# The first slot of the experts: its first weights loaded and halved during attention

## Chip, cores and metric

One NeuronCore of a Trainium2 chip runs the program. The metric is the device time in microseconds, the median of several runs.

## The reference

Attention with a memory (B = 4, H = 8, S = 576, D = 64), an expert layer that gives each of 2304 tokens to one of 8 experts (512 to 1024 to 512), and a dense layer (512 to 2048 to 512), all fp32:

```python
local = softmax(causal(q @ k.T / 8)) @ v
mem_out = (phi(q) @ M_prev) / (phi(q) @ z_prev + 1e-6)
x = sigmoid(beta) * mem_out + (1 - sigmoid(beta)) * local   # -> (2304, 512)
e_idx = argmax(x @ w_gate)                                  # one expert a token
y = gate_w * sigmoid(x @ w_output_gate)[e] * (relu(x @ w1[e]) @ w2[e])
h = y @ w_in
out = (h - tanh(h)) @ w_out
```

## The kernel before

Each fp32 product is made of three matmuls: both factors are halved into a high and a low part (`split`, L48: ScalarE casts the high part, L50, and VectorE subtracts it, L51), and high by high, high by low and low by high are added up in PSUM.

*Attention.* 16 pairs: four batches of four pairs of heads. In a pair PE (TensorE) transposes q and k (`tq`, `tk`, `tt`), makes scores (`sc`, and `sct` for the last query block, L448), and later the transposes of the weights (`g`, `ta`, `tb`), the products with v (`l`) and the projection to the tile `xb` that is stored to the table `xd`; VectorE masks the scores and takes their row maxima (`a`, `nm`, L455), ScalarE takes the exponentials (L476, L487). The order on each engine is not that of the code. Every operation is put into a `Plan` with a due time, its cost on each engine that can do it, and what it reads and writes; a list scheduler walks through them by due time and writes out one fixed order for each engine. The due times come from tables: `DUE` by kind of operation, shifted by `PERIOD` a pair, `ROUTE` for the steps of the router, `DUE0` for what is done once: the gates (VectorE, L110 to L124), the 0/1 patterns and number rows of the router (`laterrt`, VectorE and GpSimd, L727 to L773), the gate weights `w160`.

*Router.* After each batch, `Router.batch` picks an expert for each token from the logits in `acc` (`mx` to `os`, L833 to L848), and counts them (`cb`, `cs`; the matmuls `rp`, L887 to L891). After the third batch, `Router.first_slot` (names `e_...`) takes the fullest expert so far, its number `e_e` (L973), gathers 256 of its tokens and halves them into `xh_first`, `xl_first`. The rest, with the last batch, is done in `Router.slots` (L1019), a generator of some ten short chunks that make the tables of all slots: the first (up to `nF`, L1060) counts the slots of each expert, the next ones write the token list of slot 0 and its expert number `ei` (L1103), the last write other tables.

*Experts.* Slot e (256 tokens, list made in attention), then twelve more slots. A slot has eight steps of 128 inner features. Step f: 12 matmuls into `ph`, Relu on ScalarE (`hh`), its remainder on VectorE (`hl`, L1301), 12 matmuls into `y`. `run_slots` (L1189) drives it: `first` and `parts2` halve a step's pieces of w1 (`ah`, `al`) and w2 (`bh`, `bl`), `load` issues two DMAs of 512 KB each for every two steps on SyncE, `ahead` keeps `first` two steps ahead. `between`, a function of the main program, runs after each step: it takes the next chunk of `Router.slots` and, later, a piece of the dense layer's conversions. In slot e, step 0:

```python
            if s.first and f == 0:
                nc.scalar.copy(s.wh, r)
                nc.gpsimd.tensor_tensor(out=s.wl, in0=r, in1=s.wh.bitcast(F32), op=ALU.subtract)
```

The number of its expert is read into SyncE by a register load that stands ahead of the last stores of `xb`; the loads of its weights stand behind those stores.

Of the kernel before, what the change touches and what calls it, by code (L numbers as in the profile page):

```python
# [276 lines left out]
DUE = {
    "mx": (-371.1, -38.4, -63.2, -4.7, -23.8, -10.4, -17.1, -329.2), "kt": (-356.8,), "nrm": (-319.8,),
    "phi": (-319.7,), "qtt": (-218.6,), "pt": (-193.0,), "ptt": (-174.7,),
    "ex": (-97.7, -29.7, -360.9, -178.0, 9.4, 9.1, -54.4, -78.3), "lt": (-66.1, -9.5), "mxt": (-65.1,),  # L280
    "cp": (-60.8, -194.3, -30.0, -48.9, -29.0), "tpt": (-49.1,), "sdt": (-48.6,), "qt": (-47.4,),
    "new": (-45.7,), "sm": (-45.7,), "loadq": (-36.0,), "consts": (-30.0,), "qexp": (-29.5,), "loadk": (-20.7,),
# [6 lines left out]
}  # L289

DUE0 = {"constsM": 33.9, "constsz": 16.3, "laterM": -165.5, "latergates": 6.8, "laterrt": 17.1, "laterw160": -25.5, "laterzeros": 23.6}

# [895 lines left out]

def run_slots(tc, c, pm, ps, rt, slots, w1, w2, x2, between):  # L1189

# [54 lines left out]
    def first(s, f):  # L1245

        nm = f"{s.n}_{f}"
        load()
        r1 = raw[s.n, f - f % 2][0]
        if s.nl == 2:  # L1250
            s.wh, s.wl = wtile(f"ah_{nm}", "wh", [P, 4, P]), wtile(f"al_{nm}", "wl", [P, 4, P])
            r = r1[:, :, (f % 2) * P:(f % 2 + 1) * P]
# [12 lines left out]

    def parts2(s, f, j):
        nonlocal used
        nm = f"{s.n}_{f}"
# [433 lines left out]
```

## Time and profile before

| what | us |
|---|---|
| median of 3 runs | 983.3 (982.25 to 983.88) |
| profiled execution | 983.37 |
| its span | 981.5 |
| attention, to the last write of `xb` | 0 to 263.38 |
| slot e, to the end of `xl` of slot 0 | 263.38 to 299.64 |
| other slots and dense layer | 299.64 to 981.5 |
| busy: PE, DVE, ACT, POOL | 924.2, 807.3, 655.7, 128.3 |

PE is TensorE's matmuls, PEld its weight loads, DVE VectorE, ACT ScalarE, POOL GpSimd, SP SyncE, SPq its DMA issues. In a timeline a row gives the start in the span, the duration, the engine, the line, the operation, output <- input, the shape, the number of equal operations, and in brackets how long the engine was idle before it and what it waited for. In a table of stretches each engine has its busy time and its instructions; the clock is the share of full speed (2.4 GHz) that TensorE was granted.

### The profile page before, as it was taken

The numbers are of one execution on the slowest core, as the hardware profiler recorded it, in microseconds if no ns is written. First come the engines' busy times: TensorE is split into PE (matmuls) and PEld (weight loads), VectorE is DVE, ScalarE is ACT, GpSimd is POOL, SyncE is SP. The second block draws the span as 40 slices with busy tenths as digits, with TensorE's granted clock in tenths as the row PEclk, the third lists the DMA queues.
The fourth block names the chain that finished last, engine by engine and source line by source line (L and its number), as shares of the span: only waits on it lengthen the run. The fifth ranks groups of instructions, "written<-read, shape, count | busy, mean of one in ns | idle before, by whom it ended". The sixth has DMA issues, their size and how long they took to land. (4 is left out here: it accounts for less than half of the span.)

```text
span 981.5 us, 16678 instructions
## 1 busy us (share of the span) xinstructions
PE 924.2 (94%) x5661; PEld 759.2 (77%) x5661; DVE 807.3 (82%) x1908; ACT 655.7 (67%) x1441; POOL 128.3 (13%) x145
## 2 busy tenths in 40 slices
PE   5899999999599999999999899999999999999996
PEld 3567666666489989989998777777887888788895
DVE  4566777868589989988888789999889888988896
ACT  4577777776346676676768467776667666665784
POOL 2433233322230001000000000001001000100000
PEclk9799999999889999999999899999999999999999
DMA  5133433431378987888988201001000000100000
GB/s 126 26 81 83 100 88 83 104 84 36 102 223 253 291 299 229 266 284 265 307 263 268 89 2 43 22 1 44 1 1 33 11 1 1 44 1 1 12 33 22
DMA packets 139117, 103.60 MB, mean 106 GB/s; under 512 B 85776, under 2 KB 120592, under 8 KB 139024
## 3 DMA queue, kind: packets, MB, share of 16 engines
q1 hardware_dynamic: 135680, 91.88, 32.0%
q0 software_dynamic: 3200, 10.58, 3.3%
q8 instruction: 46, 0.75, 0.3%
q14 instruction: 47, 0.39, 0.1%
q10 hardware_dynamic: 144, 0.00, 0.0%
HBM read 92.93 MB, written 9.51 MB: 104 GB/s over the span
## 5 line engine op out<-in xcount | busy, mean ns | idle before, releaser
L1469 PE MATMUL og<-wouth,fgl 128*128 128x512 f32 x288 | 115.4, 401 | 8.0 <-DVE fgl L1480 7.9
L1469 PE MATMUL og<-woutl,fgh 128*128 128x512 f32 x288 | 114.8, 399 | 0.0
L1553 ACT ACTIVATE fu<-fph 128x512 f32<-128x512 f32 (+1 forms) x80 | 44.4, 555 | 104.9 <-PE fph L1520 81.2
L1469 PE MATMUL og<-wouth,fgh 128*128 128x512 f32 x288 | 113.5, 394 | 0.2
L1520 PE MATMUL fph<-fxh,fwh 128*128 128x512 f32 (+1 forms) x256 | 93.8, 369 | 4.8 <-ACT fxh L50 4.8
L1520 PE MATMUL fph<-fxh,fwl 128*128 128x512 f32 (+1 forms) x256 | 93.2, 367 | 0.0
L1520 PE MATMUL fph<-fxl,fwh 128*128 128x512 f32 (+1 forms) x256 | 92.9, 365 | 0.0
L476 ACT ACTIVATE a<-a,nm 128x128 f32<-128x128 f32 (+3 forms) x128 | 71.6, 567 | 21.4 <-DVE nm L455 21.4
L1487 POOL DMA_INDIRECT out_dram<-ob,olist x18 | 18.9, 1049 | 458.8 <-ACT ob L1485 246.9
L1555 DVE SCALAR_TENSOR_TENSOR fs<-fs,fu 128x512 f32<-128x512 f32 (+1 forms) x80 | 50.9, 637 | 29.7 <-ACT fs L1554 29.3
L1469 PEld LDWEIGHTS og<-wouth,fgl 128*128 128x128 f32 x288 | 54.3, 189 | 25.0 <-DVE fgl L1480 13.3
L51 DVE TENSOR_TENSOR bl<-r,bh 128x512 fp32r<-128x512 f32 x96 | 64.5, 686 | 11.1 <-ACT bh L50 10.7
L1308 PE MATMUL y<-hh,bh 128*128 128x256 f32 x256 | 71.8, 280 | 0.0
L1308 PE MATMUL y<-hh,bl 128*128 128x256 f32 x256 | 71.4, 279 | 0.0
L1308 PE MATMUL y<-hl,bh 128*128 128x256 f32 x256 | 71.4, 279 | 0.0
L455 DVE CUSTOM_DVE_ANT_0 a<-sc,cm 128x128 f32<-128x128 f32 (+3 forms) x128 | 57.5, 487 | 8.9 <-PE sc L435 8.6
L51 DVE TENSOR_TENSOR al<-r,ah 128x512 fp32r<-128x512 f32 x96 | 64.4, 685 | 0.1
L1469 PEld LDWEIGHTS og<-wouth,fgh 128*128 128x128 f32 x288 | 54.3, 189 | 12.7 <-ACT fgh L1475 1.4
L1469 PEld LDWEIGHTS og<-woutl,fgh 128*128 128x128 f32 x288 | 54.3, 189 | 12.1 <-DVE woutl L51 0.5
L1566 DVE TENSOR_TENSOR ft<-fph,ft 128x512 f32<-128x512 f32 (+1 forms) x80 | 50.9, 636 | 11.6 <-ACT ft L1564 11.2
L1300 ACT ACTIVATE hh<-ph 128x256 fp32r<-128x256 f32 x64 | 24.7, 385 | 52.6 <-PE ph L1295 52.6
L1520 PEld LDWEIGHTS fph<-fxh,fwh 128*128 128x128 f32 x256 | 48.9, 191 | 13.9 <-ACT fxh L50 5.7
(372 smaller groups left out, 2797.8 us busy)
## 6 DMA issues: line engine op xcount, KB each, us to landing
r<-in_moe_w_dram SPq DMA_DIRECT2D x96, 512.0 KB
d<-in_moe_w_in_dram SPq DMA_DIRECT2D x16, 512.0 KB
d<-in_moe_w_out_dram SPq DMA_DIRECT2D x16, 512.0 KB
qr<-in_q_dram SPq DMA_DIRECT2D x32, 128.0 KB
kr<-in_k_dram SPq DMA_DIRECT2D x32, 128.0 KB
vr<-in_v_dram SPq DMA_DIRECT2D x32, 128.0 KB
xd<-xb SPq DMA_DIRECT2D x32, 128.0 KB
r_e<-in_moe_w_dram SPq DMA_DIRECT2D x8, 512.0 KB
```

What stands on the lines that cost most here:

```text
L51: nc.vector.tensor_tensor(out=lo, in0=src, in1=hi.bitcast(F32), op=ALU.subtract)
L455: nc.vector.tensor_tensor_reduce(out=y, in0=x, in1=mask, scale=-0.125, scalar=init, op0=ALU.add, op1=ALU.min, accum_out=out)
L476: nc.scalar.activation(a, a, AF.Exp, bias=s.nm[:, o:o + 1], scale=-1.0, accum_out=s.sum[:, i, j:j + 1])
L1300: nc.scalar.activation(hh, hv, AF.Relu)
L1308: nc.tensor.matmul(s.y[d // 2][:, d % 2, :], st[:, d * P:(d + 1) * P], mv, start=f == 0 and m == 0 and d % 2 == 0, stop=f == 7 and m == 2, ...
L1469: nc.tensor.matmul(og[ci][t], st[:, ts], mv, start=f == 0 and m == 0, stop=f == 15 and m == 2)
L1487: sc = nc.gpsimd.indirect_dma_start(out=out, out_offset=bass.IndirectOffsetOnAxis(ap=perm[:, i:i + 1], axis=0), in_=ob, in_offset=None).ins
L1520: nc.tensor.matmul(h, st[:, k, :], xp[ci, k][o], start=m == 0, stop=m == 11)
L1553: nc.scalar.activation(u, h, AF.Square)
L1555: nc.vector.scalar_tensor_tensor(out=s, in0=s, scalar=KA, in1=u, op0=ALU.add, op1=ALU.mult)
L1566: nc.vector.tensor_tensor(out=th, in0=h, in1=th, op=ALU.subtract)
```

## The change

A new class `Early` makes 12 tiles in a pool `wide` that lies in the memory of the later tiles `wout` of the dense layer: w1 and w2 of inner features 0 to 255 of slot e's expert, and their high and low parts. As soon as the expert number is known, SyncE loads them (four DMAs of 256 KB), and four casts and four subtracts halve them before attention ends. `run_slots` makes no pieces for steps 0 and 1 of slot e and takes `pre.a`, `pre.b`; the halving on GpSimd is gone. `between` is not called ahead of slot e and does nothing after its step 0, so that the chunks of the router start after step 1 and end two steps later, the last two in slot 0. All due times are new.

```diff
-PERIOD = 19.44
-ROUTE = 1.48
+PERIOD = 20.2
+ROUTE = 1.35
 DUE = {
...
-DUE0 = {"constsM": 33.9, "constsz": 16.3, "laterM": -165.5, "latergates": 6.8, "laterrt": 17.1, "laterw160": -25.5, "laterzeros": 23.6}
+DUE0 = {"constsM": 28.5, "constsz": 3.9, "laterM": -151.2, "latergates": -23.5, "laterrt": -12.9, "laterw160": -28.9, "laterzeros": 27.7}
...
+            if nm == "e_f6":
+                plan.add(at, f"e_load_{b}", (("SP", 2.0),), lambda e: pre.load(rt.v["e"]), r=w, w=["ew"], lat=6.0)
+                for i, (e_, d_, f_) in enumerate(pre.steps):
+                    plan.add(NPAIR * B * PERIOD + 7.0 + 0.5 * i, f"e_w{i}_{b}", ((e_, d_),), lambda e, f=f_: f(), r=["ew"] + ([f"ew{i - 1}"] if i % 2 else []), w=[f"ew{i}"])
...
+class Early:
+    def __init__(self, tc, pool, w1, w2):
...
+        self.r = [[t(f"er{n}_{f}", F32, (P, 4, P) if n == 1 else (P, DM)) for f in range(2)] for n in (1, 2)]
+        self.a = [[t(f"ea{a}_{f}", F32R, (P, 4, P)) for a in "hl"] for f in range(2)]
+        self.b = [[t(f"eb{a}_{f}", F32R) for a in "hl"] for f in range(2)]
+        self.steps = []
+        for f in range(2):
+            for x, (h, l) in ((self.r[0][f], self.a[f]), (self.r[1][f], self.b[f])):
+                self.steps.append(("ACT", 0.6, lambda x=x, h=h: nc.scalar.copy(h, x)))
+                self.steps.append(("DVE", 0.7, lambda x=x, h=h, l=l: nc.vector.tensor_tensor(
+                    out=l, in0=x, in1=h.bitcast(F32), op=ALU.subtract)))
+    def load(self, t):
+        e = nc.sync.value_load(t[0:1, :], min_val=0, max_val=E - 1)
+        for f in range(2):
+            nc.sync.dma_start(self.r[0][f], self.w1[bass.ds(e, 1), :, f * P:f * P + P].rearrange("a (k p) f -> p (a k) f", p=P))
+            nc.sync.dma_start(self.r[1][f], self.w2[bass.ds(e, 1), f * P:f * P + P, :].rearrange("a p f -> p (a f)"))
...
-    pieces = [(s, f) for s in slots for f in range(0, 8, 2)]
+    pieces = [(s, f) for s in slots for f in range(0, 8, 2) if f or not s.first]
...
+        if s.first and f < 2:
+            s.w1[f] = pre.a[f]
+            return
...
-            if s.first and f == 0:
-                nc.scalar.copy(s.wh, r)
-                nc.gpsimd.tensor_tensor(out=s.wl, in0=r, in1=s.wh.bitcast(F32), op=ALU.subtract)
-            else:
-                split(nc, s.wh, s.wl, r)
+            split(nc, s.wh, s.wl, r)
...
+        if s.first and f < 2:
+            return pre.b[f]
...
-    between(slots[0], 0, -1, None, None)
...
-            if i == 0 or i == 1 and f % 2:
+            if i == 0 and f or i == 1 and f % 2:
```

How this moves instructions, at three places. First VectorE around the first masks of attention (`a`, `nm`; `ptc` and `ir` are the last constants of the router). Before, in front of pair 1's first mask:

```order
L751 CAST thr<-thr_i 128x18
L766 CAST ptc<-io_t 128x40
L767 MEMSET ptc 64x4x2
L771 CAST ir<-io_r 128x128
L370 SCALAR_TENSOR_TENSOR ph_181<-qr_165,ph_181 128x640
L455 ISA a_0_140,nm_137<-sc_1_357,cm 128x128
L455 ISA nm_137 128x1
```

With the change, in front of pair 0's first mask (the gates `sel` to `ft` and the other constants stand directly ahead of these rows, and nothing but the setting up of masks and gate weights ahead of those):

```order
L754 CAST thr<-thr_i 128x18
L769 CAST ptc<-io_t 128x40
L770 MEMSET ptc 64x4x2
L774 CAST ir<-io_r 128x128
L416 TENSOR_TENSOR qtt_264<-tt_262,bm 128x128
L454 ISA a_1_144,nm_140<-sc_0_280,cm 128x256
L454 ISA nm_140 128x1
```

Gates and router constants have moved from between pair 0 and pair 1 to ahead of pair 0. Second, SyncE's queue at the end of attention (`xd<-xb` are the stores of the last batch, `r_e` slot e's weights as they are loaded). Before:

```order
L1196 TENSOR_LOAD e_e
L1196 ISA x2
L643 DMA xd<-xb_118 128x4x64 x2
L643 DMA xd<-xb_118 64x64 x2
L643 DMA xd<-xb_118 128x4x64 x2
L643 DMA xd<-xb_118 64x64 x2
L1240 ISA
L1240 DMA r_e_3334<-in_moe_w_dram 128x4x256
L1242 ISA
```

With the change (`er_0`, `er_1` are the raw pieces of steps 0 and 1):

```order
L1201 ISA
L1201 DMA er_0_87<-in_moe_w_dram 128x4x128
L1202 ISA
L1202 DMA er_0_89<-in_moe_w_dram 128x512
L1201 ISA
L1201 DMA er_1_88<-in_moe_w_dram 128x4x128
L1202 ISA
L1202 DMA er_1_90<-in_moe_w_dram 128x512
L1227 TENSOR_LOAD e_e
L1227 ISA x2
L642 DMA xd<-xb_133 128x4x64 x2
L642 DMA xd<-xb_133 64x64 x2
```

The four early loads stand ahead of the last stores; behind those the first `r_e` load is now that of step 2. Third, VectorE around the count `cb` and the running count `cs` of the last batch, which the list-making chain starts from (`os` is the chosen output gate logit, `rank` and `rlo` belong to the chain). Before:

```order
L853 TENSOR_REDUCE cb_3350<-oh 128x8
L848 TENSOR_REDUCE os_3272<-oe_3268 128x5
L854 TENSOR_TENSOR cs<-cs,cb_3350 128x8
L897 TENSOR_TENSOR rs_3364<-rp_3355,oh 128x40
L898 TENSOR_REDUCE rank<-rs_3364 128x5
L899 CAST ri_3367<-rank 128x5
L900 TENSOR_SCALAR rj_3369<-ri_3367 128x5
L901 TENSOR_SCALAR ri_3367<-ri_3367 128x5
L902 CAST rhi<-rj_3369 128x5
L903 CAST rlo<-ri_3367 128x5
```

With the change:

```order
L851 TENSOR_REDUCE os_3308<-oe_3304 128x5
L1333 SCALAR_TENSOR_TENSOR hl_e_3396<-ph_e_3382,hh_e_3395 128x256
L51 TENSOR_TENSOR al_e_3413<-r_e_3370,ah_e_3412 128x512
L1333 SCALAR_TENSOR_TENSOR hl_e_3417<-ph_e_3399,hh_e_3416 128x256
L856 TENSOR_REDUCE cb_3434<-oh 128x8
L857 TENSOR_TENSOR cs<-cs,cb_3434 128x8
```

The subtract `al_e` (step 2's weights) and two remainders `hl_e` (steps 0 and 1) now stand ahead of the count `cb`, and so of all chunks of the router.

## Rows read from the trace of the kernel before

**Rows 1.** Stretches: us, busy PE, PEld, DVE, ACT, POOL, clock, DMA share, GB/s.

```profile
16.81:34.88 18.07, 12.22 (x45) 6.46 (x46) 11.28 (x61) 8.25 (x25) 8.86 (x34) 0.76 0.37 83
34.88:50.60 15.72, 15.72 (x95) 10.74 (x95) 9.37 (x37) 10.79 (x31) 5.14 (x4) 0.84 0.11 24
50.60:236.61 186.01, 184.20 (x1303) 125.71 (x1303) 138.41 (x547) 140.77 (x409) 59.01 (x42) 1.00 0.38 84
263.38:299.64 36.26, 28.44 (x230) 27.02 (x231) 31.63 (x103) 15.31 (x33) 9.13 (x10) 0.86 0.77 241
299.64:322.80 23.16, 22.84 (x208) 22.59 (x207) 20.35 (x40) 15.70 (x33) 2.75 (x4) 1.00 0.77 237
```

**Rows 2.** Timeline of PE, first pairs: start, duration, operation, [idle before it <- releaser].

```profile
16.81 2.02 PE L448 MATMUL sct<-kt,qtt 128*128 128x512 f32 x2
...
32.83 1.64 PE L435 MATMUL sc<-kt,qt 64*128 64x384 f32 x2 [3.91 <-DVE nm L455]
...
50.60 1.08 PE L448 MATMUL sct<-kt,qtt 128*128 128x512 f32 x2
```

**Rows 3.** Stretches around the fall of the clock, columns as in rows 1.

```profile
19.40:26.26 6.86, 4.93 (x31) 2.86 (x29) 6.26 (x39) 5.92 (x16) 0.83 (x8) 1.00 0.45 101
26.26:34.88 8.62, 4.71 (x11) 2.15 (x11) 4.49 (x22) 2.33 (x9) 6.15 (x24) 0.50 0.14 31
```

**Rows 4.** Timelines of ACT, SP's queue and DVE at the start.

```profile
6.20 0.74 ACT L367 ACTIVATE ph<-qr 128x640 f32<-128x640 f32 x1
...
4.02 0.59 SPq L135 DMA_DIRECT2D w<-in_moe_w_gate_dram  x1
...
6.64 1.15 SPq L352 DMA_DIRECT2D kr<-in_k_dram  x2
...
20.57 0.16 DVE L114 TENSOR_SCALAR g<-g 128x8 f32<-128x8 f32 x1
...
22.09 0.46 DVE L124 COPY ft<-g 128x8 f32<-128x8 f32 x5
...
25.32 0.11 DVE L735 CAST ie<-io_e 128x8 f32<-128x8 int32 x1
...
29.16 0.23 DVE L771 CAST ir<-io_r 128x128 f32<-128x128 int32 x1 [0.21 <-POOL io_r L769]
```

**Rows 5.** Timeline of PE, rank matmul of batch 0.

```profile
117.13 0.19 PE L887 MATMUL rp<-ohb,tri 128*128 128x40 bf16 x1 [0.61 <-DVE ohb L847]
```

**Rows 6.** Stretch before the last write of `xb`, and timeline of DVE there.

```profile
244.00:263.38 19.38, 15.33 (x113) 11.94 (x109) 8.72 (x31) 7.46 (x18) 5.55 (x7) 0.91 0.32 74
...
245.57 0.14 DVE L973 TENSOR_SCALAR e_e<-e_fm 128x1 int32<-128x1 f32 x1
```

**Rows 7.** Timelines of SP's queue and ACT, first weights of slot e.

```profile
265.79 0.40 SPq L1240 DMA_DIRECT2D r_e<-in_moe_w_dram  x1
...
269.24 0.62 ACT L1254 CAST ah_e<-r_e 128x512 fp32r<-128x512 f32 x1 [5.89 <-DMA r_e<-in_moe_w_dram]
```

**Rows 8.** Timeline of DVE in slot e.

```profile
266.78 0.22 DVE L853 TENSOR_REDUCE cb<-oh 128x8 f32<-128x40 f32 x1
...
270.21 0.15 DVE L1060 COPY nF<-end 128x1 f32<-128x1 f32 x1
271.52 0.69 DVE L51 TENSOR_TENSOR bl_e<-r_e,bh_e 128x512 fp32r<-128x512 f32 x1 [1.15 <-ACT bh_e L50]
...
274.21 0.43 DVE L1301 SCALAR_TENSOR_TENSOR hl_e<-ph_e,hh_e 128x256 fp32r<-128x256 f32 x1 [1.40 <-DMA r_e<-in_moe_w_dram]
...
294.21 0.57 DVE L1125 TENSOR_TENSOR rn<-rn,va 128x400 f32<-128x400 f32 x1
...
295.71 0.68 DVE L51 TENSOR_TENSOR bl_e<-r_e,bh_e 128x512 fp32r<-128x512 f32 x1
...
297.25 0.82 DVE L794 TENSOR_TENSOR list_eq<-tk,ir 128x640 bf16<-128x640 f32 x1
298.35 1.29 DVE L51 TENSOR_TENSOR xl<-xt,xh 128x512 fp32r<-128x512 f32 x2 [0.28 <-ACT xh L50]
```

More of the change, by code (lines that the diff above doesn't have):

```diff
@@ L273, with attention @@
 QORDER = (1, 3, 2, 0)
-PERIOD = 19.44
-ROUTE = 1.48
+PERIOD = 20.2
+ROUTE = 1.35
 DUE = {
[L278 to L282, printed above, removed]
[6 rows of a table removed]
-}
-DUE0 = {"constsM": 33.9, "constsz": 16.3, "laterM": -165.5, "latergates": 6.8, "laterrt": 17.1, "laterw160": -25.5, "laterzeros": 23.6}
-def attention(tc, c, pl, ps, src, M_prev, z_prev, rt):
+    "phi": (-111.9,), "ex": (-102.0, -50.1, -50.1, -62.7, 9.7, 9.5, -102.1, -14.1), "xw": (-90.6, 26.0),
+    "cp": (-88.9, 7.5, -12.7, -45.5, -46.0), "ptt": (-87.6,), "qt": (-82.1,), "pt": (-68.5,), "new": (-67.4,),
+    "mxt": (-66.6,), "sct": (-61.0,), "loadq": (-49.3,), "qtt": (-46.7,),
+    "mx": (-44.9, -43.4, -32.7, -70.7, -89.3, -15.8, -25.6, 13.8), "lt": (-42.3, -44.3), "sdt": (-39.6,),
+    "ktt": (-34.9,), "tpt": (-31.9,), "loadk": (-31.1,), "consts": (-30.0,), "qexp": (-29.8,), "mv": (-15.0,),
+    "tq": (-14.8,), "tp": (-13.3,), "pz": (-12.1,), "tk": (-12.1,), "tt": (-11.7,), "kt": (-11.1,),
+    "cb": (-9.0,), "avM": (0.4,), "sc0": (0.4,), "qmin": (0.5,), "nrm": (5.0,), "sc2": (5.1,), "loadv": (5.2,),
[3 rows of a table added]
+}
+DUE0 = {"constsM": 28.5, "constsz": 3.9, "laterM": -151.2, "latergates": -23.5, "laterrt": -12.9, "laterw160": -28.9, "laterzeros": 27.7}
+def attention(tc, c, pl, ps, src, M_prev, z_prev, rt, pre):
     nc = tc.nc
@@ L1171, with t @@
 AH2 = 0
+class Early:
+    def __init__(self, tc, pool, w1, w2):
+        nc = self.nc = tc.nc
+        def t(name, dt, shape=(P, DM)):
+            return pool.tile(list(shape), dt, tag="wout", bufs=17, name=name)
+        self.w1, self.w2 = w1, w2
+        self.r = [[t(f"er{n}_{f}", F32, (P, 4, P) if n == 1 else (P, DM)) for f in range(2)] for n in (1, 2)]
[8 more added lines that the diff above has]
+    def load(self, t):
+        nc = self.nc
+        e = nc.sync.value_load(t[0:1, :], min_val=0, max_val=E - 1)
+        for f in range(2):
+            nc.sync.dma_start(self.r[0][f], self.w1[bass.ds(e, 1), :, f * P:f * P + P].rearrange("a (k p) f -> p (a k) f", p=P))
+            nc.sync.dma_start(self.r[1][f], self.w2[bass.ds(e, 1), f * P:f * P + P, :].rearrange("a p f -> p (a f)"))
 class Slot:
@@ L1186, in __init__, with run_slots @@
         self.w = self.nl * P
-def run_slots(tc, c, pm, ps, rt, slots, w1, w2, x2, between):
+def run_slots(tc, c, pm, ps, rt, slots, w1, w2, x2, between, pre=None):
     nc = tc.nc
@@ L1430, with ffn @@
 C3, GA, AL, KA = -0.018684760036080127, -2.6849726608097573, -0.09139710496091785, 6.635977108247196
-def ffn(tc, c, bp, pf, ps, x2, win, wout, perm, out, cst, rest):
+def ffn(tc, c, wp, pf, ps, x2, win, wout, perm, out, cst, rest):
     nc = tc.nc
@@ L1533, in ffn @@
         if 0 < i < 17:
-            vl = bp.tile([P, DM], F32R, tag="wout", bufs=17, name=f"woutl_{i - 1}")
+            vl = wp.tile([P, DM], F32R, tag="wout", bufs=17, name=f"woutl_{i - 1}")
             split(nc, wouth[:, i - 1, :], vl, wout[i - 1])
@@ L1608 @@
     rt = Router(tc, c, rp, xd)
+    wp = ctx.enter_context(tc.tile_pool(name="wide", bufs=1, side="right", reuse_waits="tile"))
+    pre = Early(tc, wp, w1, w2)
     with ExitStack() as st:
@@ L1612 @@
         make_consts(tc, c, pl, beta, w_gate, w_ogate)
-        late = attention(tc, c, pl, ps, (q, k, v), M_prev, z_prev, rt)
+        late = attention(tc, c, pl, ps, (q, k, v), M_prev, z_prev, rt, pre)
     ps = early.enter_context(tc.tile_pool(name="mps", bufs=4, space=PSUM, reuse_waits="tile"))
@@ L1617 @@
     win = [bp.tile([P, 4, P], F32, name=f"win_{f}") for f in range(16)]
-    wout = [bp.tile([P, DM], F32, tag="wout", bufs=17, name=f"wout_{f}") for f in range(16)]
+    wout = [wp.tile([P, DM], F32, tag="wout", bufs=17, name=f"wout_{f}") for f in range(16)]
     cst = bp.tile([P, 2], F32, name="cst")
@@ L1657 @@
         with tc.manual_schedule():
-            run_slots(tc, c, pm, ps, rt, stat, w1, w2, x2, between)
+            run_slots(tc, c, pm, ps, rt, stat, w1, w2, x2, between, pre)
             for _ in order:
@@ L1669 @@
         with tc.manual_schedule(engines={nc.tensor.engine, nc.vector.engine, nc.scalar.engine}):
-            ffn(tc, c, bp, pf, ps, x2, win, wout, rt.perm, out, cst, [units[j] for j in (28, 30, 27, 29, 31)])
+            ffn(tc, c, wp, pf, ps, x2, win, wout, rt.perm, out, cst, [units[j] for j in (28, 30, 27, 29, 31)])
 _INS = ["q", "k", "v", "M_prev", "z_prev", "beta", "moe_w_gate", "moe_w_output_gate",
```

9 rows, old and new, of the table DUE are left out of this document.

## Prediction

> **What bounds the kernel now.** I read the stretches first (busy time of each engine between two marks of the program), then TensorE's timeline, then VectorE's, and the queue of SyncE where a load is late. All times are of one profiled execution: 983.37 us, of which 981.5 are the span and 1.87 lie around it; the median of the three runs is 983.3, so the sum needs no correction. A difference of 0.2% (2 us) is about what a measurement of this kernel can tell from none.
>
> Attention is a loop of 16 head pairs. The 128x512 matmuls `sct`, two in each pair, mark its beat. From the third `sct` (50.60) to the sixteenth (236.61) PE is busy 184.20 of 186.01 us: PE is the bound, and only 1.81 us could be won by waiting less [rows 1]. The two pairs before it are different. From the first `sct` (16.81) to the second (34.88) PE works 12.22 of 18.07 us at a mean clock of 0.76, and the next pair takes 15.72 without a gap at 0.84 [rows 1]. So the start holds 5.85 us of waiting, of which 3.91 is one wait for VectorE's row maxima `nm` [rows 2], and PE runs at half clock (1.2 of 2.4 GHz) in part of it: 0.50 from 26.26 on [rows 3]. Matmuls before 19.4 are also slow: the first `sct` took 2.02 us, the later one 1.08 [rows 2].
>
> The other loose place is slot e, the first 256 tokens of the experts. From the last write of `xb` (263.38) to the end of slot 0's first halving (299.64) VectorE works 31.63 of 36.26 us and PE 28.44 at a clock of 0.86 [rows 1]: VectorE is the bound there. After that, in slot 0, PE is busy 22.84 of 23.16 and VectorE 20.35 [rows 1].
>
> **The change part by part.** *The order of the start.* The 3.91 us wait comes from what VectorE does before pair 1's first mask: the gates (20.57 to 22.55, 2.0 us), then the router's constants, which go back and forth with GpSimd from 25.32 to 29.39 (4.07 us) [rows 4]. The new order puts both ahead of pair 0's first mask. There VectorE has nothing else: the gate's exponential can follow ScalarE's first `ph`, which ends at 6.94 [rows 4], so gates and constants run from about 7.1 to 7.1 + 2.0 + 4.07 = 13.2. At that time PE still waits for its own input: the first k was issued at 6.64, behind four loads of gate weights that begin at 4.02 [rows 4]; now it goes ahead of them, 2.6 us earlier. PE's chain from k to the first `sct` could end 2.6 us sooner, VectorE's 13.2 plus its copy `qtt` allows about 14.8: I take 14.8, that is 2.0 sooner.
>
> From the first to the second `sct`: of 12.22 us busy, 18.07 x 0.24 x 2 = 8.7 us of the stretch ran at half clock. Less the wait of 3.91, 4.8 us of matmuls were slow; at full clock they take 2.4. The 2.0 us by which the pair starts earlier now lie before 19.4, where matmuls are slow, and cost 1.0. Of the three small waits (1.94 together) I keep one, 0.7. So 12.22 - 2.4 + 1.0 + 0.7 = 11.5, and the second `sct` comes at 26.3. The next pair had 15.72 x 0.16 x 2 = 5.0 us at half clock; without that 15.72 - 2.5 = 13.2, third `sct` at 39.5 in place of 50.60: **-11.1**. Bounds: if PE runs at half clock as long as before, 13.6 us more, 6.8 of it are given back (-4.3); if no wait stays, -12.
>
> What keeps the clock up? The rows show only that it fell to 0.50 at 26.26, after 6.86 us in which PE was busy 4.93 with three short waits, and ahead of the long one [rows 3]. The Trainium skill, "TensorE: Matmul & The Clock Gate", "HAM oscillation — how this bites in real kernels", blames waits between groups of matmuls for the fall. By it the denser start holds the clock and -11.1 stands; by the row alone the clock may fall again without a long wait, and -4.3 is the sum's term. I take -11.1, since the new stretch lacks the waits, and keep the other as a rival.
>
> *Router operations of batches 0 to 2.* They cost PE a wait for `ohb` of about 0.6 us each [rows 5]. The new due times spread them otherwise. At most the whole idle 1.81 us goes [rows 1], at least nothing: **-1.0**.
>
> *Early weights.* Four loads of 256 KB go out on SyncE as soon as the expert is known, 245.57 [rows 6], behind the value register and ahead of the last `xb` stores, which wait for VectorE anyway. Four casts of 0.62 us on ScalarE and four subtracts of 0.69 on VectorE follow. From 244 to 263.38 VectorE works 8.72 of 19.38 us and ScalarE 7.46 [rows 6]: 2.8 and 2.5 us more fit. I cost them at **0**; without that cover they would cost up to 2.8.
>
> *Slot e.* Count from the last `xb` write. Before, the first load of weights went out at +2.4 behind the `xb` stores, and ScalarE's cast began at +5.86 [rows 7]; everything of slot e began there. Now steps 0 and 1 need no load, so PE may begin at about 0. But step 2's weights still stand behind the same stores and arrive at +5.9: cast +6.5, subtract `al` +7.2. VectorE's queue holds this `al` between `hl` of step 0 and `hl` of step 1, ahead of the count `cb`. So the list-making chain, which ran from 266.78 to 270.36 (3.58 us) beside the wait, now follows it: +7.2 + 0.3 + 3.6 = +11.1 for `nF`, where it was +7.0 [rows 8]. From `nF` to `xl` it took 298.35 - 270.36 = 27.99. Out of this go two waits for weights, 1.15 and 1.40; two steps' `bl`, `al`, `hl` at 1.54 a step (295.71 to 297.25); and two chunks of list-making that now lie in slot 0, 1.50 (294.21 to 295.71) and 0.82 [rows 8]. 27.99 - 2.55 - 3.08 - 2.32 = 20.0, so `xl` ends at 11.1 + 20.0 + 1.29 = +32.4. The number of slot 0's expert is now made two steps later, and a load takes 3.45 us from issue to cast [rows 7]; I add 1.4 for waiting on it: +33.8 against +36.26 before: **-2.4**. So most of PE's head start of six us is lost to VectorE. Bounds: -6.5 if only PE's start counts, +4 if the list chain (3.6) finds no cover and the load wait is double.
>
> *Slot 0.* Two chunks, 2.32 us of VectorE, join 20.35 busy of 23.16 [rows 1]: between 0 and +2.3, value **+1.2**.
>
> *Clock in slot e.* PE waits between steps 1 and 2 for about as long as it did before step 0, and 36.26 x 0.14 x 2 = 10.2 us of this stretch were at half clock already [rows 1]. A slower stretch may show behind VectorE: **+1.0**, from 0 to +6.
>
> The sum is -11.1 - 1.0 - 2.4 + 1.2 + 1.0 = -12.3, so 983.37 - 12.3 = **971.1 us**. With its terms' nearer bounds this case reaches from 966 to 976.
>
> **The rivals.** *B, the clock falls all the same at the start.* For it: the fall at 26.26 came without a long wait [rows 3]. Against: PE has fewer gaps. The start's term is then -4.3 and the time 977.9; in the worst case, half clock from the first `sct` to 40, it is -1.5 and 980.7. *C, slot e runs on a half clock.* Its PE work, 28.44 less half of 10.2, is 23.3 us at full and 47 at half clock; steps 2 to 7 at half need 35 us after +7.2, against the 26.6 that VectorE takes. Most of that excess, +6, gives 977. For it: the long PE wait now cuts slot e in two. Against: VectorE leaves PE the slack. *D, slower: the new order makes PE wait in every pair.* The period in the planner was raised from 19.44 to 20.2 and all due times differ; a cast or mask that comes late in one pair is late in 13. It decides from 12.3 / 13 = 0.95 us a pair; today the wait is 1.81 / 13 = 0.14 [rows 1]. At 1.25 a pair the time is 971.1 + 16.3 = 987.4. Against: the mix of copies on ScalarE and VectorE stays nearly the same, and VectorE's busy share in this stretch is only 138.41 of 186.01 [rows 1]. *E, it does not do what it says.* The early weights help nothing, since VectorE bounds slot e, and the constants wait for something else at the start: 983.
>
> **How the numbers follow.** Forecast 0.58, B 0.20, C 0.09, D 0.08, E 0.05. The range takes in the forecast and B and C but for their far ends: 966 to 980.5. Faster by over 0.2%: forecast, B, C, 0.87; within 0.2%: E, 0.05; slower: D, 0.08.
>
> **What the profile after would show.** The third `sct` near 39.5, no wait of 3.91 for `nm`, and a granted clock near 1.00 between 26 and 40 (B: 0.50). About 14.2 us from `sct` to `sct` later (D: over 15). The four early casts and subtracts in the gap before the last `xb`. In slot e PE's first `ph_e` about at the last `xb` write, a wait for `hl` or `al` of some 3 us near +4 to +7, and `xl` ending near +34 (C: PE clock 0.5 until +20). The prediction is wrong if the third `sct` comes after 46, or if slot 0 begins later than +36 after the last `xb`.

## The result, and the profile after

The changed kernel takes 973.75 us (median of 4 runs, 971.69 to 974.65) where the kernel before takes 983.39 (982.25 to 983.88): a ratio of 0.9908, 95% interval 0.9894 to 0.9922, or some 9 us less. The profiled execution took 971.69 us, its span 969.8. That is 2 us below the median, at a mean clock of 0.990 where the three other runs have 0.982 to 0.988; the readings below go by marks inside the profiles.

First the start. TensorE's timeline with the change, to be read against [rows 2]:

```profile
14.19 1.65 PE L434 MATMUL sc<-kt,qt 64*128 64x384 f32 x2 [2.73 <-DVE nm L454]
15.77 2.07 PE L447 MATMUL sct<-kt,qtt 128*128 128x512 f32 x2
...
24.17 0.98 PE L498 MATMUL g<-idf,a 128*128 128x128 f32 x7 [0.95 <-ACT a L475]
...
25.93 1.13 PE L447 MATMUL sct<-kt,qtt 128*128 128x512 f32 x2
...
39.14 1.12 PE L447 MATMUL sct<-kt,qtt 128*128 128x512 f32 x2
```

and the stretches between the first, second and third `sct`, up to the sixteenth, and slot e (columns as in [rows 1]):

```profile
15.77:25.93 10.16, 9.21 (x46) 5.77 (x45) 8.14 (x32) 7.15 (x24) 4.47 (x4) 1.00 0.69 157
25.93:39.14 13.21, 13.21 (x95) 8.81 (x93) 9.35 (x36) 10.27 (x30) 4.80 (x9) 1.00 0.22 49
39.14:223.69 184.55, 183.84 (x1307) 125.81 (x1305) 146.04 (x544) 143.28 (x414) 59.65 (x43) 1.00 0.38 85
252.61:288.37 35.76, 27.93 (x221) 26.69 (x221) 27.37 (x92) 12.47 (x27) 7.83 (x9) 0.91 0.61 194
```

The third `sct` begins at 39.14 (before 50.60). The 3.91 us wait for `nm` of pair 1 is gone; what is left is 2.73 us ahead of the first `sct`, where VectorE now makes the router's constants, and 0.95 behind it. The granted clock is 1.00 from 15.77 to 39.14, where it was 0.76 and 0.84 [rows 1]. Up to about 19 us this record says too much, before as after: the first `sct` took 2.07 us, as long as one at 0.50 in e3 below (2.08), the third 1.12. The loop after it is 1.46 us shorter (184.55 against 186.01), and the wait for the rank matmul fell from 0.61 [rows 5] to 0.21; it comes three times in the loop, once a batch:

```profile
105.55 0.19 PE L890 MATMUL rp<-ohb,tri 128*128 128x40 bf16 x1 [0.21 <-DVE ohb L850]
```

Then the end of attention, first PE, then GpSimd:

```profile
241.82 0.47 PE L568 MATMUL l<-idf,p 128*128 128x128 f32 x1 [2.75 <-POOL p L555]
...
238.04 1.18 POOL L961 DMA_INDIRECT e_xg<-xd,e_li  x1 [11.47 <-DMA er<-in_moe_w_dram]
239.53 0.95 POOL L961 DMA_INDIRECT e_xg<-xd,e_li  x1 [0.30 <-issue]
240.50 1.26 POOL L555 TENSOR_TENSOR p<-ph,gn 128x640 f32<-128x640 f32 x1
```

PE waits 2.75 us for GpSimd's last `p`, which stands behind both gathers of slot e's tokens. From the sixteenth `sct` to the last `xb` write it takes 28.92 us, where it took 26.77 (236.61 to 263.38).

Slot e, VectorE's timeline, then the load and the cast that it waits for, to be read against [rows 7, 8], and PE's first matmul:

```profile
255.66 0.41 DVE L1333 SCALAR_TENSOR_TENSOR hl_e<-ph_e,hh_e 128x256 fp32r<-128x256 f32 x1
259.31 0.69 DVE L51 TENSOR_TENSOR al_e<-r_e,ah_e 128x512 fp32r<-128x512 f32 x1 [3.24 <-ACT ah_e L50]
259.92 0.42 DVE L1333 SCALAR_TENSOR_TENSOR hl_e<-ph_e,hh_e 128x256 fp32r<-128x256 f32 x1
260.25 0.21 DVE L856 TENSOR_REDUCE cb<-oh 128x8 f32<-128x40 f32 x1
...
264.01 0.15 DVE L1063 COPY nF<-end 128x1 f32<-128x1 f32 x1
...
283.89 0.69 DVE L51 TENSOR_TENSOR al<-r,ah 128x512 fp32r<-128x512 f32 x1 [2.29 <-ACT ah L50]
...
287.68 0.69 DVE L51 TENSOR_TENSOR xl<-xt,xh 128x512 fp32r<-128x512 f32 x1 [0.16 <-ACT xh L50]
...
255.02 0.39 SPq L1271 DMA_DIRECT2D r_e<-in_moe_w_dram  x1
...
258.66 0.62 ACT L50 CAST ah_e<-r_e 128x512 fp32r<-128x512 f32 x1 [4.40 <-DMA r_e<-in_moe_w_dram]
...
252.10 0.38 PE L1327 MATMUL ph_e<-xh_first,eah 128*128 128x256 f32 x1 [0.58 <-DVE xl_first L1019]
```

PE's first matmul of slot e in the kernel before:

```profile
269.91 0.58 PE L1295 MATMUL ph_e<-xh_first,ah_e 128*128 128x256 f32 x1 [2.49 <-ACT ah_e L1254]
```

PE's first `ph_e` begins at 252.10, 0.5 us before the last `xb` write (252.61); before, it came 6.5 us after it. But VectorE waits 3.24 us for step 2's cast, whose load went out at +2.4 as before, and only then comes the count `cb` and the list chain: `nF` ends at +11.6. At the end of slot e it waits 2.29 us for the first weights of slot 0. `xl` ends at +35.8, 0.5 us earlier than before (+36.26).

The marks of both traces together (us; `x<-y_e` is the copy that ends slot e, the dense layer begins with its first `fph`):

| mark | before | after | shift |
|---|---|---|---|
| first, second `sct` | 16.81, 34.88 | 15.77, 25.93 | -1.0, -9.0 |
| third `sct` | 50.60 | 39.14 | -11.5 |
| sixteenth `sct` | 236.61 | 223.69 | -12.9 |
| last `xb` write ends | 263.38 | 252.61 | -10.8 |
| `x<-y_e` | 299.59 | 289.50 | -10.1 |
| copy that ends slot 0 | 327.20 | 318.49 | -8.7 |
| dense layer begins | 560.9 | 553.1 | -7.8 |
| end of the span | 981.5 | 969.8 | -11.7 |

So attention's order gained 12.9 us, 5.1 of them were given back between the sixteenth `sct` and the dense layer, and the dense layer, whose code is the same, became 3.9 us shorter. Of these 3.9, 2.4 lie in its steady stretch (258.6 and 256.1 us, see e8) and 1.3 in the stretch ahead of that (97.3 and 96.0 us at a mean clock of 0.96 and 0.97). The latter takes 96.0 to 97.7 us in the fourteen profiles here, in no order that follows the edits, so this part counts as scatter.

### The profile page after: what moved, and what is told of

The parts are those of the page before. It is cut to its first block, busy times and chain, and to the rows that moved or that the text cites. A ratio compares the mean times of both kernels' runs of the same rounds, so it can differ in the third digit from the quotient of the medians.

```text
span 969.8 us, 16684 instructions
## 1 busy us (share of the span) xinstructions
PE 916.9 (95%) x5661; PEld 757.7 (78%) x5661; DVE 814.7 (84%) x1905; ACT 657.3 (68%) x1445; POOL 127.5 (13%) x144
## 5 line engine op out<-in xcount | busy, mean ns | idle before, releaser
L1500 PE MATMUL og<-woutl,fgh 128*128 128x512 f32 x288 | 112.4, 390 | 0.0
L475 ACT ACTIVATE a<-a,nm 128x256 f32<-128x256 f32 (+3 forms) x128 | 70.4, 552 | 18.4 <-DVE nm L454 18.3
L1500 PEld LDWEIGHTS og<-wouth,fgh 128*128 128x128 f32 x288 | 54.1, 188 | 11.5 <-ACT fgh L1506 1.5
L1500 PEld LDWEIGHTS og<-woutl,fgh 128*128 128x128 f32 x288 | 54.1, 188 | 11.1 <-DVE woutl L51 0.5
L454 DVE CUSTOM_DVE_ANT_0 a<-sc,cm 128x256 f32<-128x256 f32 (+3 forms) x128 | 57.4, 485 | 5.6 <-PE sc L434 4.6
L50 ACT CAST ah<-r 128x512 fp32r<-128x512 f32 x96 | 58.2, 624 | 4.9 <-DMA r<-in_moe_w_dram 4.9
```

The costliest lines, as they stand in the source:

```text
L50: nc.scalar.copy(hi, src)
L454: nc.vector.tensor_tensor_reduce(out=y, in0=x, in1=mask, scale=-0.125, scalar=init, op0=ALU.add, op1=ALU.min, accum_out=out)
L475: nc.scalar.activation(a, a, AF.Exp, bias=s.nm[:, o:o + 1], scale=-1.0, accum_out=s.sum[:, i, j:j + 1])
L1500: nc.tensor.matmul(og[ci][t], st[:, ts], mv, start=f == 0 and m == 0, stop=f == 15 and m == 2)
```

## The experiments

All kernels start from the changed one unless it is said otherwise. Ratios are to the kernel before on the same chip (its median there 981.8 to 983.4). "Slots" runs from `x<-y_e` to the dense layer.

| kernel | ratio, 95% interval | third `sct` | sixteenth | `xb` after it | slot e | slots | dense begins | dense layer |
|---|---|---|---|---|---|---|---|---|
| before | 1 | 50.60 | 236.61 | +26.8 | 36.2 | 261.3 | 560.9 | 420.6 |
| changed | 0.9908 (0.9894 to 0.9922) | 39.14 | 223.69 | +28.9 | 36.9 | 263.6 | 553.1 | 416.7 |
| e1, due times alone | 0.9904 (0.9882 to 0.9926) | 38.91 | 223.44 | +27.9 | 36.4 | 261.1 | 548.8 | 421.1 |
| e2, early weights alone | 1.0021 (1.0008 to 1.0033) | 49.99 | 236.00 | +28.1 | 34.8 | 264.9 | 563.8 | 417.6 |
| e3, constants back | 0.9938 (0.9914 to 0.9963) | 43.53 | 228.05 | +29.2 | 34.9 | 263.7 | 555.8 | 418.3 |
| e9, old DUE0 | 0.9971 (0.9961 to 0.9981) | 46.24 | 230.78 | +29.2 | 37.1 | 264.1 | 561.2 | 417.0 |
| e4, `p` first | 0.9872 (0.9842 to 0.9903) | 39.01 | 223.57 | +25.9 | 38.0 | 263.8 | 551.3 | 418.1 |
| e5, steps 2, 3 early | 0.9887 (0.9870 to 0.9903) | 38.96 | 223.53 | +29.2 | 34.9 | 263.7 | 551.3 | 418.2 |
| e6, chunks from step 0 | 0.9803 (0.9785 to 0.9820) | 39.21 | 223.72 | +30.5 | 30.5 | 260.0 | 544.7 | 417.4 |
| e11, chunks ahead of step 0 | 0.9834 (0.9819 to 0.9849) | 39.09 | 223.61 | +29.2 | 32.0 | 262.0 | 546.8 | 416.9 |
| e10, e2 with chunks from step 0 | 0.9911 (0.9896 to 0.9926) | 49.28 | 235.33 | +27.6 | 31.0 | 259.9 | 553.9 | 417.6 |
| e8, before with the pool alone | 0.9970 (0.9959 to 0.9980) | 50.87 | 236.89 | +26.8 | 36.4 | 261.2 | 561.2 | 417.9 |
| e7, e6 and e4 | 0.9765 (0.9748 to 0.9781) | 39.11 | 223.68 | +26.1 | 31.5 | 260.3 | 541.6 | 417.5 |
| b2, e7 and e5 | 0.9810 (0.9797 to 0.9824) | 39.09 | 223.65 | +29.7 | 31.0 | 260.3 | 544.6 | 418.3 |

**Which half gains.** My theory: the new due times carry the whole gain. The rival: the early weights carry part of it. e1 is the kernel before with the new tables and nothing else, e2 the changed kernel with the old tables.

e1, against the kernel before (and so on through `ROUTE`, `DUE`, `DUE0`):

```diff
-PERIOD = 19.44
+PERIOD = 20.2
...
```

e2, against the changed kernel, likewise:

```diff
-PERIOD = 20.2
+PERIOD = 19.44
...
```

> The kernel before with the new due times alone, no early weights, and the router chunks where they were. Theory (the new order is the whole gain, the early weights give back some): third sct at 39.1 and sixteenth at 223.7 as in the changed kernel, slot e as long as before (36.3 us from the last xb write to the end of xl), no 2.75 us wait of PE at the end of attention, dense layer begins near 547.6 where the changed kernel begins it at 553.1; time 968 to 971, below the changed kernel. Rival (the early weights carry part of the gain): dense layer begins at 555 to 558, time 976 to 978.

> The changed kernel with the old due times: early weights and later router chunks alone. Theory (the early weights do not pay, since step 2's load, VectorE and the later expert number bound slot e): third sct at 50.6 as before, dense layer begins 2 to 4 us later than before (563 to 565), time 985 to 987. Rival (PE's earlier start in slot e counts): 2.4 to 6.5 us faster than before, 977 to 981.

In e1 the dense layer begins 12.1 us earlier than before, in e2 2.9 us later: the due times gain, the early weights as they stand (with the chunks of the router two steps later) cost 2.9 us alone and 4.3 on top of the new order (553.1 against 548.8). The rivals fell. Two things were missed. e1's wait for `p` at the end of attention is there (2.75 us), so it belongs to the due times and not to the early loads. And e1 is no faster overall than the change, because its dense layer takes 421.1 and not 416.7.

Behind this wait, equally long in both, the granted clock is 1.00 in e1 and 0.50 in the changed kernel (columns as in [rows 1], e1 first):

```profile
242.00:244.00 2.00, 2.00 (x16) 1.36 (x15) 0.66 (x1) 0.70 (x2) 1.57 (x4) 1.00 0.06 19
```

```profile
242.00:244.00 2.00, 2.00 (x9) 2.00 (x9) 0.00 (x0) 0.76 (x3) 1.58 (x2) 0.50 0.25 98
```

From the end of the wait to the last products `l` by `w` it is 6.6 us in e1 and 7.6 in the changed kernel, and this is the 1.1 us by which its last `xb` write comes later after the sixteenth `sct` (+28.9, +27.9). What brings the clock down in one and not in the other no run shows. In e2 attention ends 1.3 us later after the sixteenth `sct` than before (+28.1, +26.8), without such a wait for `p`. VectorE in e2:

```profile
253.55 0.69 DVE L1195 TENSOR_TENSOR eal<-er,eah 128x512 fp32r<-128x512 f32 x1 [2.84 <-ACT eah L1194]
254.16 0.15 DVE L991 SCALAR_TENSOR_TENSOR e_li<-e_pp,e_l 128x2 int32<-128x2 f32 x1
```

The first early subtract stands ahead of `e_li`, the token list that the gather waits for, and itself waits 2.84 us for its cast, so the gather goes out at 254.61 and not at 251.82 as before, and PE waits 0.82 us for its tokens ahead of the last `xo`.

**The place of the constants.** e3 moves the router's constants back between pair 0 and pair 1, e9 restores the old `DUE0`, gates and all.

e3:

```diff
-DUE0 = {"constsM": 28.5, "constsz": 3.9, "laterM": -151.2, "latergates": -23.5, "laterrt": -12.9, "laterw160": -28.9, "laterzeros": 27.7}
+DUE0 = {"constsM": 28.5, "constsz": 3.9, "laterM": -151.2, "latergates": -23.5, "laterrt": 17.1, "laterw160": -28.9, "laterzeros": 27.7}
```

e9:

```diff
-DUE0 = {"constsM": 28.5, "constsz": 3.9, "laterM": -151.2, "latergates": -23.5, "laterrt": -12.9, "laterw160": -28.9, "laterzeros": 27.7}
+DUE0 = {"constsM": 33.9, "constsz": 16.3, "laterM": -165.5, "latergates": 6.8, "laterrt": 17.1, "laterw160": -25.5, "laterzeros": 23.6}
```

> The changed kernel with the router's constants back between pair 0 and pair 1; the order of the other engines is unchanged. Theory (the place of these constants is the start's gain, and the granted clock falls with the wait): a wait of about 4 us of PE for nm returns, clock 0.50 for some 10 us, third sct at 47 to 50, time 981 to 984. Rival (only the wait itself comes back, the clock stays at 1.00): third sct at 43, time 977 to 978.

> The changed kernel with the old DUE0: gates and router constants both behind pair 0's masks, the k load still ahead of the gate weights. Theory (gates and constants together are what PE waits for at the start): third sct at 47 to 50, close to the 50.6 of before, a wait of PE for nm of about 4 us with half clock behind it. Rival (most of the start's gain beyond the 4.4 us of the constants comes from the other order, of loads and matmuls): third sct at 43 to 45 as with the constants alone moved back.

PE's timeline in e3, and stretches around its wait of 3.31 us (columns as in [rows 1]):

```profile
12.54 2.07 PE L447 MATMUL sct<-kt,qtt 128*128 128x512 f32 x2
...
26.14 1.09 PE L498 MATMUL g<-idf,a 128*128 128x128 f32 x4 [3.31 <-DVE att L301]
...
28.74 2.08 PE L447 MATMUL sct<-kt,qtt 128*128 128x512 f32 x2
...
43.53 1.12 PE L447 MATMUL sct<-kt,qtt 128*128 128x512 f32 x2
```

```profile
22.50:25.00 2.50, 0.33 (x3) 0.09 (x1) 0.78 (x5) 0.00 (x0) 1.37 (x12) 1.00 0.63 144
...
26.10:28.74 2.64, 2.60 (x8) 1.22 (x8) 1.99 (x10) 2.32 (x10) 1.70 (x2) 0.50 0.00 0
```

The same two views of e9:

```profile
12.38 2.07 PE L447 MATMUL sct<-kt,qtt 128*128 128x512 f32 x2
...
30.00 1.64 PE L434 MATMUL sc<-kt,qt 64*128 64x384 f32 x2 [6.93 <-DVE nm L454]
31.58 2.07 PE L447 MATMUL sct<-kt,qtt 128*128 128x512 f32 x2
...
46.24 1.12 PE L447 MATMUL sct<-kt,qtt 128*128 128x512 f32 x2
```

```profile
25.00:30.00 5.00, 0.00 (x0) 0.00 (x0) 2.69 (x19) 0.44 (x2) 2.88 (x21) 0.50 0.00 0
30.00:35.00 5.00, 5.00 (x14) 2.89 (x15) 4.03 (x11) 2.96 (x12) 4.06 (x8) 0.54 0.26 58
```

e3's third `sct` came at 43.5, where its rival put it: the constants alone are worth 4.4 us. But the rival's reason, a clock that stays at 1.00, does not hold. The clock does fall during the 3.31 us wait (1.00, then 0.50; the `sct` at 28.74 takes 2.08 us and not 1.13), but the first `sct` comes 3.2 us earlier without the constants ahead of it, and that pays for part of it. With all of `DUE0` back a wait of 6.93 us returns, half clock with it (0.50, 0.54), and 7.1 us are lost: the third `sct` at 46.24 lies between the theory's 47 to 50 and the rival's 43 to 45, nearer to the theory. Even so the first `sct` stands at 12.4 and not at 16.81: k goes out ahead of the gate weights in this kernel too. So of the 11.5 us, 4.4 are the constants, 2.7 the gates and the rest of `DUE0`, and 4.4 the rest of the order, where the first `sct` gained as much.

**The tail of attention.** e4 shifts the due time of the gather by 10 us, so that GpSimd makes the last `p` first; on the other engines only what hangs on it moves.

```diff
-            plan.add(at, f"{name}_{b}", ((eng, dur),), lambda e, f=f: f(), r=r, w=w, new=new,
+            plan.add(at + (10.0 if nm == "e_gather" else 0.0), f"{name}_{b}", ((eng, dur),), lambda e, f=f: f(), r=r, w=w, new=new,
```

> The changed kernel with GpSimd's last p ahead of the gather of slot e's tokens. Theory (the 2.75 us wait of PE for p at the end of attention is on the path): last xb write 2.5 us earlier after the sixteenth sct, all later marks 2 to 2.5 us earlier, time about 971.3. Rival (the gather, now 1.3 us later, holds up xl_first, and slot e begins no earlier): same time as the changed kernel, 973.7.

The wait is gone, and with it the half clock behind it (1.00 from 238 to 254). The last `xb` write comes 3.1 us earlier, and 1.9 are left at the dense layer: slot e grew by 1.1, since VectorE's waits for step 2's and slot 0's weights grew to 3.98 and 2.79 us.

**What slot e waits for.** e5 loads steps 2 and 3 early too (raw, in four more tiles of the pool); e6 lets the router's chunks begin after step 0; e11 puts them ahead of step 0, where they were.

e5 (the loads in `Early.load` run over four steps as well):

```diff
-        self.r = [[t(f"er{n}_{f}", F32, (P, 4, P) if n == 1 else (P, DM)) for f in range(2)] for n in (1, 2)]
+        self.r = [[t(f"er{n}_{f}", F32, (P, 4, P) if n == 1 else (P, DM)) for f in range(4)] for n in (1, 2)]
...
-    pieces = [(s, f) for s in slots for f in range(0, 8, 2) if f or not s.first]
+    pieces = [(s, f) for s in slots for f in range(0, 8, 2) if f > 2 or not s.first]
...
+            split(nc, s.wh, s.wl, pre.r[0][f])
...
+            split(nc, vh, vl, pre.r[1][f])
```

e6:

```diff
-            if i == 0 and f or i == 1 and f % 2:
+            if i == 0 or i == 1 and f % 2:
```

e11 is e6 with this line ahead of the loop over the steps:

```diff
+    between(slots[0], 0, -1, None, None)
```

> The changed kernel, with the raw weights of steps 2 and 3 also loaded during attention (four more early loads, halved in slot e as before). Theory (step 2's load behind the xb stores is what VectorE waits 3.24 us for, with the list chain queued behind it): the wait is gone, end of xl near +33 from the last xb write in place of +35.8, dense layer begins 2 to 3 us earlier (550.5). Rival (slot 0's first weights, for which VectorE waits 2.29 us at the end of slot e, set its length): xl at +35.8 as before, dense layer at 553.

> The changed kernel with the router's chunks begun after step 0 of slot e and not after step 1. Theory (the later chunks are what the early weights cost): the list chain of 3.6 us fills the 3.24 us wait for al, slot 0's expert number comes one step earlier so that the 2.29 us wait goes, and one chunk moves from slot 0 back into slot e: dense layer begins 4 to 5 us earlier than in the changed kernel (548 to 549), time about 969. Rival (PE then waits for cs between steps 0 and 1 and gives it back): within 1 us of the changed kernel, 552 to 554.

> The changed kernel with the router's chunks begun ahead of step 0 of slot e, where they were before the change. Theory (hl of step 0 then stands behind the list chain of 3.6 us on VectorE, and PE's first matmuls behind the wait for cs): slot e 1 to 3 us longer than with the chunks after step 0, dense layer begins at 546 to 548. Rival (the list and the expert number one step earlier win more than that): 542 to 543.5.

e6 gains 8.4 us at the dense layer from one condition, about twice what its theory said. VectorE's timeline in e6:

```profile
257.19 0.41 DVE L1333 SCALAR_TENSOR_TENSOR hl_e<-ph_e,hh_e 128x256 fp32r<-128x256 f32 x1
257.52 0.21 DVE L856 TENSOR_REDUCE cb<-oh 128x8 f32<-128x40 f32 x1
...
260.85 0.15 DVE L1063 COPY nF<-end 128x1 f32<-128x1 f32 x1
261.02 0.69 DVE L51 TENSOR_TENSOR al_e<-r_e,ah_e 128x512 fp32r<-128x512 f32 x1
261.63 0.42 DVE L1333 SCALAR_TENSOR_TENSOR hl_e<-ph_e,hh_e 128x256 fp32r<-128x256 f32 x1
...
274.42 0.18 DVE L1106 TENSOR_SCALAR ei<-ei 128x20 int32<-128x20 int32 x1
...
281.02 0.69 DVE L51 TENSOR_TENSOR al<-r,ah 128x512 fp32r<-128x512 f32 x1
```

The list chain (`cb` 257.52 to `nF` 261.00) now runs while step 2's weights arrive, and `al_e` follows it without a wait. Slot 0's expert number is ready at 274.60, +20.4 from the last `xb` write; in the changed kernel it was +25.3 (277.75 and 0.18 more). The wait of 2.29 us for slot 0's weights is gone. Slot e is 6.4 us shorter and the slots behind it 3.6, while the tail of attention was 1.5 longer in this profile (`l` by `vr` took 4.31 us and not 2.81 behind the wait for `p`: half clock). e5 gave 1.9 us and shows why not more: the first wait is gone, but VectorE then waits 3.10 us for slot 0's weights, and `xl` ends at +34.0, between the theory's +33 and the rival's +35.8. e11 lies between, as expected: with the chain ahead of `hl` of step 0, slot e takes 1.5 us more than in e6. It is still 6.3 us better at the dense layer than the changed kernel, so that much is what moving the chunks two steps later cost.

**Do the early weights pay with the chunks in place?**

This is e6's edit in e2:

```diff
-            if i == 0 and f or i == 1 and f % 2:
+            if i == 0 or i == 1 and f % 2:
```

> The kernel with the old due times and the early weights, and the router's chunks begun after step 0. Theory (the early weights pay once the chunks don't wait for step 1): the dense layer begins some 8 us earlier than with the chunks after step 1 (563.8), at 555 to 556, 5 us before the 560.9 of the kernel before; time 974 to 976. Rival (the place of the chunks helps only under the new order): 560 to 563.

The dense layer begins at 553.9 under the old due times: 9.9 us better than e2, 7.0 better than the kernel before, a little more than expected. Against the kernel before, e10 changes two things, the weights and the place of the chunks (after step 0, not ahead of it). What the weights alone do, e11 against e1 shows: the same due times, the chunks ahead of step 0 in both, and the dense layer begins at 546.8 with early weights and 548.8 without. So they pay, with 2.0 us: slot e is 4.4 us shorter, the end of attention 1.3 and the slots 0.9 longer. Chunks after step 0 without early weights were not run, so how much of the rest needs both is open.

**The dense layer.** e8 is the kernel before with `wout` and `woutl` in a pool `wide` of their own, opened where the change opens it.

```diff
+    wp = ctx.enter_context(tc.tile_pool(name="wide", bufs=1, side="right", reuse_waits="tile"))
...
-    wout = [bp.tile([P, DM], F32, tag="wout", bufs=17, name=f"wout_{f}") for f in range(16)]
+    wout = [wp.tile([P, DM], F32, tag="wout", bufs=17, name=f"wout_{f}") for f in range(16)]
-            vl = bp.tile([P, DM], F32R, tag="wout", bufs=17, name=f"woutl_{i - 1}")
+            vl = wp.tile([P, DM], F32R, tag="wout", bufs=17, name=f"woutl_{i - 1}")
```

> The kernel before with one thing changed: the tiles wout and woutl of the dense layer in a pool of their own, opened where the change opens it. Theory (their place in memory makes the dense layer's steady stretch 256.1 us where it is 258.6 without the pool, as the five profiles so far show): all marks up to the dense layer as before, the stretch 256.1, time 2.5 us below before. Rival (something else of the change does it, such as the order in which the tiles are taken): 258.6, time as before.

The costliest groups of matmuls in the dense layer's steady stretch (from the first to the last matmul of `fx` by `fwh`), before and in e8, with busy time and mean ns:

```profile
L1469 PE MATMUL og<-wouth,fgl 128*128 128x512 f32 x185 | 73.3, 396 | 1.3 <-DVE fgl L1480 1.3
L1469 PE MATMUL og<-woutl,fgh 128*128 128x512 f32 x184 | 73.0, 397 | 0.0
L1469 PE MATMUL og<-wouth,fgh 128*128 128x512 f32 x184 | 71.9, 391 | 0.0
```

```profile
L1469 PE MATMUL og<-wouth,fgl 128*128 128x512 f32 x185 | 72.3, 391 | 1.4 <-DVE fgl L1480 1.4
L1469 PE MATMUL og<-wouth,fgh 128*128 128x512 f32 x184 | 71.6, 389 | 0.0
L1469 PE MATMUL og<-woutl,fgh 128*128 128x512 f32 x184 | 71.6, 389 | 0.0
```

The stretch takes 256.1 us with the pool and 258.6 without, at a granted clock of 1.00 both times; so it does throughout: 256.1 to 256.3 in the eleven kernels here that have the pool and in the change, 258.6 in the two without. The matmuls on `woutl` take 389 ns and not 397; those of `wouth` by `fgl`, which stand right behind them and read no tile of the pool, 391 and not 396. That is 2.5 us of the change's gain that has nothing to do with early weights. Whether it is the place of `wout` and `woutl` themselves or of tiles that moved with them, e8 does not tell.

**The best version.** e7 is e6 and e4 together, b2 is e7 with e5's loads.

> Chunks after step 0 and GpSimd's last p ahead of the gather, both in the changed kernel. Theory (the two are independent): last xb write 3 us earlier after the sixteenth sct, dense layer begins at 542 to 543 in place of 544.7, time about 962. Rival (the later gather holds up the lists or xl_first): no earlier than 544.7, time 963.9.

> As the previous kernel, and the raw weights of steps 2 and 3 loaded early as well. Theory (with the chunks after step 0 the list chain fills the wait for step 2's weights, so that their load no longer counts): within 1 us of the previous kernel. Rival (the load still counts): 1.5 to 3 us faster than it.

e7 took 958.8 us (ratio 0.9765), the fastest, 3 us less than its theory said: it keeps the early weights, starts the chunks after step 0 and makes the last `p` first. b2 is slower by 3 us at the dense layer, which neither theory said. GpSimd's timeline in e7 and in b2:

```profile
238.32 1.19 POOL L961 DMA_INDIRECT e_xg<-xd,e_li  x1 [0.17 <-DMA er<-in_moe_w_dram]
239.81 0.95 POOL L961 DMA_INDIRECT e_xg<-xd,e_li  x1 [0.30 <-issue]
244.15 2.03 POOL L923 TENSOR_TENSOR e_xg<-e_xg 128x512 f32<-128x512 f32 x2 [3.38 <-DMA e_xg<-xd,e_li]
```

```profile
238.31 1.19 POOL L961 DMA_INDIRECT e_xg<-xd,e_li  x1 [0.17 <-DMA er<-in_moe_w_dram]
239.80 0.95 POOL L961 DMA_INDIRECT e_xg<-xd,e_li  x1 [0.30 <-issue]
246.58 1.03 POOL L923 TENSOR_TENSOR e_xg<-e_xg 128x512 f32<-128x512 f32 x1 [5.83 <-DMA e_xg<-xd,e_li]
```

The gather of slot e's tokens is issued at the same time, but lands 2.4 us later with eight raw loads of 256 KB ahead of it than with four; PE then waits 3.24 us for it, and the last `xb` write is 3.6 us later.

## Why the prediction was right or wrong

The forecast of 971.1 us lies 2.7 below the measured 973.75, and this lies inside the range of 966 to 980.5. Point by point:

- *The start, -11.1.* Measured -11.5; the second and third `sct` were forecast at 26.3 and 39.5 and came at 25.9 and 39.1, with the clock at 1.00. The mechanism held (e9: wait and half clock come back together), but its shares were not as told: the constants alone carry 4.4 us (e3), the gates and the rest of `DUE0` 2.7, and the k load and the rest of the order another 4.4. The first `sct` was put at 14.8 and came at 15.8: VectorE was through with the constants at 13.18, as worked out, but between them and the `sct` stand the masks and PE's `sc` of 1.65 us, which the sum left out.
- *The clock.* In e3 and e9 the clock falls from 1.00 to 0.50 within a wait of 3.31 and 6.93 us, in the kernel before it fell at 26.26 [rows 3] after three waits of 0.54, 0.66 and 0.73 us, and the changed kernel, with one of 0.95 us between its first and third `sct`, keeps 1.00. The rule of the Trainium skill ("TensorE: Matmul & The Clock Gate", "HAM oscillation — how this bites in real kernels") that waits between groups of matmuls bring the clock down gave -11.1 for the start, the row alone -4.3; the start sides with the rule. The length of a single wait does not settle it, though: behind 2.75 us the clock was 1.00 in e1 and 0.50 in the changed kernel.
- *Router operations, -1.0.* Measured -1.46, from waits of 0.21 in place of about 0.6.
- *Early weights at 0.* The casts and subtracts were hidden in the changed kernel, as said (in e2 they were not). Yet the stretch from the sixteenth `sct` to the last `xb` write grew by 2.1 us. What the sentence left out is GpSimd's queue: the last `p` behind two gathers, 2.75 us of PE. The order on that engine shows it, and the prediction did not speak of that engine there. It comes from the due times, which make 1.1 of the 2.1 us (e1); the other 1.1 is half clock behind the wait, which no term held either.
- *Slot e, -2.4.* Measured -0.5 to the end of `xl`. The wait for step 2's weights (3.24 us) and `nF` at +11.6 (forecast +11.1) came about as worked out; the wait for slot 0's first weights was sized at 1.4 and is 2.29, VectorE's waits for `xh` are 0.77 where they were 0.28, and it waits another 1.12 for PE at the end of slot e, which makes +0.7 at `x<-y_e`. So this term, 2 to 3 us off, had the order of the work right and the waits behind it too short.
- *Slot 0, +1.2.* Measured +1.4. Another 0.9 us was lost in the slots behind it and not forecast.
- *Clock in slot e, +1.0.* Not seen as a cost: 0.91 in this stretch against 0.86.
- *The dense layer, no term.* It gave 2.5 us by the place of `wout` (e8). Without this the time would have been about 976, still in the range: the terms behind the sixteenth `sct` were too kind by some 5 us (-0.2 forecast, +5.1 measured), and an effect that I had not thought of gave half back. That the forecast came so near is in this part luck.

Of the rivals, B (clock), D (waits in every pair: `sct` follows `sct` in 14.2 us, 184.55 / 13, not over 15) and E as a whole are out. One half of E came true: the early weights, as they stand, do not help (e1, e2). C did not show. What I did not list is the strongest thing that the runs found behind attention: the chunks two steps later cost 6.3 us against their old place (e11), and 8 to 10 against the place after step 0 (e6, e10). The sum contains it in parts, without asking what slot e would be if the chain stayed in the gap.

## What to carry to other kernels

When a load is taken off the path, look at what the engine that waits next has queued behind its new wait; here the long router chain stood behind a wait that it could have filled, and one condition was worth as much as the whole change. A list of due times that is made anew also moves the engines that one does not look at: check every queue at the seams, GpSimd's too. And measure a change by marks in the trace, part by part, since an untouched layer can shift by as much as the edit.

## What the runs showed of the hardware

The dense layer's matmuls on `woutl`, which is their moving operand, took 397 ns with these tiles in one place of the memory and 389 in another, at the same granted clock of 1.00, and the steady stretch 258.6 and 256.1 to 256.3 us, in all fourteen profiles without an exception. Of the 2.5 us, 1.4 are theirs, and most of the rest is that of the matmuls right behind them; which property of the place does it was not tried. Four more loads of 256 KB ahead of a gather made it land 2.4 us later (b2). Behind the same wait of 2.75 us the granted clock was 1.00 in one kernel (e1) and 0.50 in another (the changed one).
